# Attention with a soft mixture of experts: a new order table for all five instruction streams

## The chip, the cores and the metric

The kernel runs on one core of a Trainium2 chip. The metric is the device time of one execution in microseconds (us), smaller is better. The median of three runs of the kernel before is 386.3 us.

## The reference

```python
scores = scale * np.matmul(q, k.transpose(0, 1, 3, 2))      # 8 batches, 8 heads, 576 x 64
mask = block_i >= block_j                                   # blocks of 64 rows
scores = np.where(mask, scores, -1000000000.0)
attn = np.exp(scores - np.max(scores, axis=-1, keepdims=True))
attn = attn / (np.sum(attn, axis=-1, keepdims=True) + 1e-09)
x = np.matmul(attn, v)                                      # heads side by side: 4608 x 512
...
logits = x @ phi                                            # 4608 x 32
d = softmax of logits over the 4608 rows; c = softmax over the 32 slots
slot_input = d.T @ x                                        # 8 experts, 4 slots each
slot_out[e] = np.maximum(slot_input[e] @ w1[e], 0.0) @ w2[e]
out = c @ slot_out
```

All values are float32. The two `softmax` lines stand for the four written-out lines of each.

## The kernel before

The 8 batches have 8 heads each; two heads make a *pair*, so there are 32 pairs, numbered m = 0 to 31, four to a batch. The 576 rows of a head are nine blocks of 64, and because of the mask a block row needs only the columns up to its own block. The kernel calls the rows by their last block: tile 7 (blocks 6 and 7, 512 columns), tile 5 (blocks 4 and 5, 384 columns), and the *small blocks* 8, 3, 2, 1 and 0, which share banks.

What is done for pair m, with the engine, the function and the name that the order table uses:

- SP loads q, k and v (`lq`, `lk`, `lv`); POOL scales k (`ks`, L276).
- PE makes the scores: `UA` tile 7 (L312, 512 columns, into the banks sc0 and sc1), `UB` the small blocks (L333, into sc8, sc0 and sc1), `UC` tile 5 (L312, 384 columns, into sc8).
- DVE takes the row maxima out of these banks (`rm..`, L347), ACT exponentiates them into SBUF and adds up the rows (`ex..`, L357), DVE inverts the sums (`z0` to `z2`, L363 and L364), POOL multiplies (`nm..`, L369).
- PE transposes the probabilities into two banks, pt_e and pt_o (L386): `g7` (16 transposes), `gc` (block 8, 10), `gd` (blocks 3 to 0, 12), `g5` (12). Each of the four groups overwrites these two banks, so each waits until the group before has been copied out: by `eg7`, `og7`, `egc`, `ogc` and so on, e for pt_e and o for pt_o (L242 on ACT, L244 on DVE).
- PE multiplies by the values: `pa` for block 8 (L434, 64 columns; it needs `egc` and `ogc` alone), `pv0` and `pv1` for the rest (L424; they need all eight copies). Both go into bank x0, and are copied into xT by `xa` (64 columns) and `xb` (512 columns).

The work is software-pipelined. In one turn of the steady state PE runs UA of pair m, `g7` of pair m-1, `pv` of pair m-2, UB of pair m, then `gc`, `gd`, `g5` and `pa` of pair m-1 around UC of pair m. The destination of the copies out of pt_e and pt_o is not doubled, so `eg7` and `og7` wait until the `pv` of the pair before has ended.

Once per batch there is work of the expert part, spread over the four turns: logits `prt0` to `prt4` (L453, L463) and their copy `elg`, running maxima `stats` and exponentials `stats2`, two turned copies `nlt` and `ndt` (L497, L498) with their copies `enl` and `disp`, x turned back `xq0`, `xq1`, `xn4` (L553) with the copies `en0a` to `en4b`, and the sums `sl` (L571, 512 columns) and `sl4` (L580) with the updates `sacc` and `sacc4`. These go through the banks x0 and x1. Where they stand between `gc` and `gd` or after `g5` or `pa`, this text calls them fillers.

All instructions are written in an order that the table `TM` sets: each step of pair m has the time m x T + TM[name], each step of batch b the time 4 x b x T + TM[name], and the steps are recorded sorted by that time. The times set the order only; on the chip every engine runs its stream in that order, and waits on semaphores. Names with `w` belong to pair 30, with `y` to pair 31, with `z` to the last batch. The table `EN` says for each copy whether ACT ("a") or DVE ("v") makes it, and with an `X` name which of the banks x0 and x1 a step uses. `FILL` puts three dummy matmuls behind `pv1` of the last pair and behind the last `sl`.

After the pairs follow the merge into siT (L694 to L696), the expert matmuls (L792, L819), and the output (L770, ten DMAs). The weights come in 32 pieces of 1 MB: 15 while the pairs run, 17 after the last load of v, into memory that the pairs have given back.

Of the kernel before, what the change touches and what calls it, by code (L numbers as in the profile page):

```python
# [45 lines left out]
for name, n in (  # L46
# [12 lines left out]
W0 = NLATE * PIECE  # L59
STEPS = (2, 2, 3, 3, 3, 3, 0)  # L60
TM = {
# [8 lines left out]
    56.559, "prt4": 57.002, "elg": 57.036, "stats": 61.554, "stats2": 62.94, "nlt": 60.569, "enl": 64.437,  # L70
# [7 lines left out]
    177.171, "slz": 214.293, "sacc4z": 228.677, "saccz": 280.777, "enlz": 179.062, "disp2z": 157.986,  # L78
    "mg6z": 241.542, "comb0z": 79.04, "comb1z": 92.334, "lqw": -27.673, "lqy": -20.712, "lkw": -27.957,
    "lky": -32.568, "lvw": -2.375, "lvy": 21.104, "ksw": -25.397, "ksy": -27.683, "UAw": -19.276, "UAy":  # L80
    -18.528, "UBw": -14.362, "UBy": -14.986, "UCw": -8.47, "UCy": -3.006, "rm70w": -18.712, "rm70y":
# [11 lines left out]
    "eg5y": 42.092, "og5w": 10.671, "og5y": 42.312, "egcw": -0.404, "egcy": 24.728, "ogcw": -0.303, "ogcy":  # L93
    14.062, "egdw": 4.267, "egdy": 31.651, "ogdw": 5.622, "ogdy": 32.008, "paw": 7.714, "pay": 27.683,
    "xbw": 13.5, "xby": 52.045, "xaw": 10.034, "xay": 34.863, "pv0": 10.742, "pv1": 10.723, "pv0w": 12.719,
    "pv1w": 12.814, "pv0y": 43.045, "pv1y": 49.055,
}
EN = {
    "xa": "v", "xb": "v", "lg": "v", "n0a": "v", "n0b": "a", "n1a": "v", "n1b": "a", "n4a": "v", "n4b": "a",
    "nl": "v", "dn": "a", "eg7": "a", "og7": "a", "eg5": "a", "og5": "a", "egc": "a", "ogc": "v", "egd":  # L100
    "a", "ogd": "v", "Xpa": 0, "Xlg": 1, "Xnl": 1, "Xnd": 0, "Xn4": 1, "Xsi": 1, "Xsi4": 0, "Xpb": 0,
    "Xlgz": 1, "Xnlz": 1, "Xndz": 0, "Xsiz": 0, "lgz": "a", "nlz": "v", "dnz": "v", "n0az": "v", "n0bz":
    "a", "n1az": "v", "n1bz": "a", "n4az": "a", "n4bz": "a", "xay": "a", "xby": "a", "eg7y": "v", "og7y":
    "a", "eg5y": "a", "og5y": "v", "egcy": "a", "ogcy": "v", "egdy": "a", "ogdy": "v", "Xpay": 0,
}
FILL = {"pv1": 3, "slz": 3}
NB = B
# [810 lines left out]
```

## Time and profile before

| what | value |
|---|---|
| runs | 386.2, 386.3, 387.93 us; median 386.3 |
| profiled execution | 387.56 us, of which the span from the first to the last instruction is 385.8 |
| busy PE, DVE, ACT, POOL | 365.4, 286.7, 278.1, 182.0 us |
| PE busy from 60 to 290 us | 226.79 of 230 us |
| scores of the small blocks (UB) of pair 2, of pair 30 | start at about 27.9 and at about 294.5 us |
| siT begins, last output is issued | 326.97 and 380.59 us |
| granted TensorE clock, mean | 0.978 |

In a timeline each row has the start, the length (from the first start to the last end of a group), engine, line, operation, what is written and read, the shape and the count; in brackets the idle time before it and what ended it. A matmul of float32 stands as two records. Ends of matmuls are modelled, so the time that PE gives to a step is read here from its start to the start of the next step. On DVE and ACT an instruction may start before the one ahead of it has ended.

### The profile page before, as it was taken

The numbers are of one execution on the slowest core, as the hardware profiler recorded it, in microseconds if no ns is written. First come the engines' busy times: TensorE is split into PE (matmuls) and PEld (weight loads), VectorE is DVE, ScalarE is ACT, GpSimd is POOL, SyncE is SP. The second block draws the span as 40 slices with busy tenths as digits, with TensorE's granted clock in tenths as the row PEclk, the third lists the DMA queues.
The fourth block names the chain that finished last, engine by engine and source line by source line (L and its number), as shares of the span: only waits on it lengthen the run. The fifth ranks groups of instructions, "written<-read, shape, count | busy, mean of one in ns | idle before, by whom it ended". The sixth has DMA issues, their size and how long they took to land.

```text
span 385.8 us, 14041 instructions
## 1 busy us (share of the span) xinstructions
PE 365.4 (95%) x5487; PEld 241.8 (63%) x5487; DVE 286.7 (74%) x851; ACT 278.1 (72%) x883; POOL 182.0 (47%) x349
## 2 busy tenths in 40 slices
PE   7799999999999999999999999999999989999974
PEld 2466677667767776777667766766776655344542
DVE  3577779887988898889888988898889866041552
ACT  2687888988898889788888888888888854211441
POOL 5465665555555555555555555555555442010000
PEclk9699999999999999999999999999999999999995
DMA  5326366353564563535636635453332289799797
GB/s 158 93 63 209 108 216 197 101 203 98 199 206 105 201 197 98 211 92 197 216 92 211 198 102 194 119 187 97 93 95 65 88 305 358 297 426 406 290 373 329
DMA packets 28786, 72.27 MB, mean 187 GB/s; under 512 B 6832, under 2 KB 15152, under 8 KB 23600
## 3 DMA queue, kind: packets, MB, share of 16 engines
q1 hardware_dynamic: 28720, 71.38, 53.7%
q8 instruction: 43, 0.70, 0.7%
q14 instruction: 23, 0.19, 0.1%
HBM read 61.93 MB, written 9.44 MB: 185 GB/s over the span
## 4 chain that ended last, share of the span: by engine, by line
PE 89%; ACT 4%; DVE 3%; issue 2%; POOL 0%; ACTq 0%; POOLq 0%; DVEq 0%
PE x L424 19%; PE sc L312 16%; PE pt_e L386 11%; PE sc L333 11%; PE x L434 6%; PE pt_o L386 5%; PE so L819 4%; PE hp L792 4%; PE o L770 3%; PE x L553 3%; PE x L453 2%; PE x L571 2%; ACT arena L242 1%; PE x L283 1%; ACT arena L357 1%
## 5 line engine op out<-in xcount | busy, mean ns | idle before, releaser
L369 POOL TENSOR_SCALAR arena<-arena,stat 128x512 f32<-128x512 f32 (+6 forms) x288 | 152.6, 548 | 135.3 <-DVE stat L364 129.8
L357 ACT ACTIVATE arena<-sc,stat 128x512 f32<-128x512 f32 (+6 forms) x288 | 154.6, 550 | 20.9 <-DVE stat L347 18.5
L347 DVE TENSOR_REDUCE stat<-sc 128x1 f32<-128x512 f32 (+6 forms) x256 | 131.6, 541 | 4.3 <-PE sc L333 1.9
L386 PEld LDWEIGHTS pt_e<-ident,arena 64*128 64x128 f32 x800 | 63.7, 139 | 47.5 <-issue 30.9
L242 ACT COPY arena<-pt_e 128x384 f32<-128x384 f32 (+2 forms) x127 | 63.4, 500 | 24.2 <-PE pt_o L386 23.0
L386 PE MATMUL pt_e<-ident,arena 64*128 64x64 f32 x800 | 74.8, 228 | 5.0 <-ACT arena L242 3.5
L424 PE MATMUL x<-arena 128*64 128x256 f32 (+2 forms) x640 | 76.1, 384 | 0.4 <-DVE arena L244 0.4
L386 PE MATMUL pt_o<-ident,arena 64*128 64x64 f32 x800 | 74.7, 228 | 0.0
L312 PE MATMUL sc<-arena 64*128 64x512 f32 (+1 forms) x256 | 67.1, 598 | 0.8 <-ACT arena L357 0.7
L386 PEld LDWEIGHTS pt_o<-ident,arena 64*128 64x128 f32 x800 | 62.7, 139 | 0.2
L357 ACT ACTIVATION_READ_ACCUMULATOR arena<-sc,stat 128x1 f32 x288 | 61.2, 212 | 0.0
L424 PEld LDWEIGHTS x<-arena 128*64 128x64 f32 x640 | 41.0, 137 | 30.6 <-issue 18.2
L333 PE MATMUL sc<-arena 64*64 64x288 f32 (+4 forms) x768 | 45.7, 344 | 2.9 <-ACT arena L357 2.9
L333 PEld LDWEIGHTS sc<-arena 64*64 64x64 f32 x768 | 38.4, 134 | 12.1 <-issue 6.3
L242 ACT COPY arena<-pt_o 128x512 f32<-128x512 f32 (+1 forms) x63 | 33.8, 537 | 10.0 <-PE x L424 9.4
L244 DVE COPY arena<-pt_o 128x320 f32<-128x320 f32 (+1 forms) x65 | 33.9, 521 | 4.9 <-PE pt_o L386 3.0
L244 DVE COPY xT<-x 128x64 f32<-128x64 f32 (+1 forms) x42 | 19.0, 453 | 12.2 <-PE x L424 11.9
L363 DVE TENSOR_SCALAR stat<-stat 128x2 f32<-128x2 f32 (+1 forms) x96 | 26.4, 275 | 2.1 <-ACT arena L357 2.1
L434 PE MATMUL x<-arena 128*64 128x64 f32 x640 | 25.7, 227 | 0.0
L312 PEld LDWEIGHTS sc<-arena 64*128 64x128 f32 x256 | 20.6, 192 | 6.3 <-issue 2.4
L276 POOL TENSOR_SCALAR arena<-arena 128x576 f32<-128x576 f32 x32 | 21.6, 674 | 3.0 <-DMA arena<-in_k 3.0
L434 PEld LDWEIGHTS x<-arena 128*64 128x64 f32 x640 | 21.2, 137 | 2.2
(142 smaller groups left out, 343.8 us busy)
## 6 DMA issues: line engine op xcount, KB each, us to landing
arena<-in_w SPq DMA_DIRECT2D x32, 1024.0 KB, 6.7
arena<-in_k SPq DMA_DIRECT2D x32, 288.0 KB, 3.7
arena<-in_q SPq DMA_DIRECT2D x32, 288.0 KB, 3.0
arena<-in_v SPq DMA_DIRECT2D x32, 256.0 KB, 3.1
out<-arena SPq DMA_DIRECT2D x8, 1024.0 KB, 4.7
arena<-in_v SPq DMA_DIRECT2D x32, 32.0 KB, 2.7
out<-arena SPq DMA_DIRECT2D x2, 512.0 KB, 4.6
arena<-in_phi SPq DMA_DIRECT2D x1, 64.0 KB, 3.1
```

The source lines that it names most:

```text
L242: nc.scalar.copy(out=out, in_=in_)
L244: nc.vector.tensor_copy(out=out, in_=in_)
L276: nc.gpsimd.tensor_scalar(out=area(f"ks{m % NQB}"), in0=area("kr"), scalar1=SCALE, scalar2=0.0, op0=ALU.mult, op1=ALU.add)
L312: nc.tensor.matmul(scores(t + str(j)), lhsT=q[r, lo:lo + 128], rhs=k[r, 0:NC[t]], start=True, stop=True)
L333: nc.tensor.matmul(o, lhsT=a, rhs=b, start=True, stop=True)
L347: nc.vector.tensor_reduce(out=st[:, 0, u:u + n], in_=sc, axis=AX.XY if x == "8" else AX.X, op=ALU.max, negate=True)
L357: nc.scalar.activation(out=pr, in_=sc, func=AF.Exp, bias=st[:, 0, u:u + 1], accum_out=st[:, 1, u:u + 1],)
L363: nc.vector.tensor_scalar(out=st[:, 2, c], in0=st[:, 1, c], scalar1=EPS, scalar2=None, op0=ALU.add)
L369: nc.gpsimd.tensor_scalar(out=pr, in0=pr, scalar1=st[:, 2, u:u + 1], scalar2=0.0, op0=ALU.mult, op1=ALU.add)
L386: nc.tensor.transpose(out=ptb[i][:, 64 * n:64 * n + 64], in_=prob(m, x)[r, 128 * c:128 * c + 128], identity=ident[r, r],)
L424: nc.tensor.matmul(xps[m, 0][64 * j:64 * j + 64, lo:hi], lhsT=vs(m)[:, j, c, :], rhs=rhs, start=a, stop=z, skip_group_check=True,)
L434: nc.tensor.matmul(xps[m, 1][64 * j:64 * j + 64, 0:64], lhsT=vs(m)[:, j, c, :], rhs=arena[:, lo:lo + 64], start=(c == 0), stop=(c == NQ - 1),)
```

## The change

`TM` and `EN` get new numbers, and T goes from 13.5 to 9.2; nothing else is changed. The lines of the changed kernel are one lower than before (L385 is L386). No function, tile or buffer is added or removed, and every instruction of the one is in the other, but for the engine of some copies. A piece of the two tables:

```diff
-    "egc": 0.999, "ogc": -0.07, "gd": 3.63, "egd": 4.561, "ogd": 4.524, "g5": 5.41, "eg5": 8.642, "og5":
-    8.288, "pa": 6.153, "xb": 11.788, "xa": 7.179, "prt0": 41.378, "prt1": 41.386, "prt2": 43.082, "prt3":
+    "T": 9.2, "lq": 8.391, "lk": 5.062, "lv": 19.959, "ks": 6.651, "UA": 10.483, "UB": 13.066, "UC": 18.108,
+    "pa": 27.331, "xb": 31.614, "xa": 27.947, "prt0": 53.039, "prt1": 53.06, "prt2": 54.239, "prt3": 59.773,
...
-    "xa": "v", "xb": "v", "lg": "v", "n0a": "v", "n0b": "a", "n1a": "v", "n1b": "a", "n4a": "v", "n4b": "a",
-    "nl": "v", "dn": "a", "eg7": "a", "og7": "a", "eg5": "a", "og5": "a", "egc": "a", "ogc": "v", "egd":
-    "a", "ogd": "v", "Xpa": 0, "Xlg": 1, "Xnl": 1, "Xnd": 0, "Xn4": 1, "Xsi": 1, "Xsi4": 0, "Xpb": 0,
+    "xa": "a", "xb": "a", "lg": "a", "n0a": "a", "n0b": "a", "n1a": "a", "n1b": "v", "n4a": "a", "n4b": "a",
+    "nl": "a", "dn": "a", "eg7": "a", "og7": "v", "eg5": "v", "og5": "a", "egc": "a", "ogc": "v", "egd":
+    "v", "ogd": "v", "Xpa": 0, "Xlg": 1, "Xpb": 0, "Xnl": 0, "Xnd": 0, "Xsi": 1, "Xsi4": 0, "Xlgz": 1,
```

What moves to another engine in a turn: `og7`, `eg5` and `egd` from ACT to DVE, `xa` and `xb` from DVE to ACT; once per batch `elg`, `en0a`, `en1a`, `en4a` and `enl` go from DVE to ACT, and `en1b` from ACT to DVE. So tile 7 and tile 5 are copied out by one engine each for pt_e and pt_o, and both halves of `gd` by DVE.

PE in one turn of the steady state, before: the last transpose of `gd`, then UC into bank sc8, `g5`, `pa` into x0, and UA of the next pair.

```order
L386 MATMUL pt_o<-ident,arena 128x64
L312 MATMUL sc_104<-arena 128x384 x2
L386 MATMUL pt_e<-ident,arena 128x64
...
L386 MATMUL pt_o<-ident,arena 128x64
L434 MATMUL x_100<-arena 64x64 x10
L312 MATMUL sc_102<-arena 128x512
```

The same place of the changed kernel, in a turn in which `xq0` stands as a filler behind `g5`:

```order
L385 MATMUL pt_o<-ident,arena 128x64
L311 MATMUL sc_104<-arena 128x384 x2
L433 MATMUL x_100<-arena 64x64 x10
L385 MATMUL pt_e<-ident,arena 128x64
...
L385 MATMUL pt_o<-ident,arena 128x64
L552 MATMUL x_100<-ident,xT_109 128x64
...
L311 MATMUL sc_102<-arena 128x512
```

The ten matmuls of `pa` have moved from behind the transposes of `g5` to ahead of them.

DVE in one turn, before (in a turn with the updates `sacc4` and `disp2`): from `xb` (the copy of x_100 into xT) over `z0`, the maximum of block 8 out of sc_104, `ogc`, the maxima of blocks 0, 1 and 2, `ogd`, to the maximum of block 3.

```order
L244 COPY xT_112<-x_100 128x512
L363 TENSOR_SCALAR stat_107<-stat_107 128x2
L364 RECIPROCAL stat_107<-stat_107 128x2
L347 TENSOR_REDUCE stat_107<-sc_104 128x1
L244 COPY arena<-pt_o 128x320
L347 TENSOR_REDUCE stat_107<-sc_102 128x1
L592 SCALAR_TENSOR_TENSOR acc_76<-acc_76,bm_1572,x_100 128x128
L512 TENSOR_TENSOR zrun<-zrun,bm_1572 128x2
L513 TENSOR_TENSOR zrun<-zrun,bm_1572 128x2
L347 TENSOR_REDUCE stat_107<-sc_103 128x1 x2
L244 COPY arena<-pt_o 128x384
L347 TENSOR_REDUCE stat_107<-sc_102 128x1
```

DVE in one turn of the changed kernel, one without updates, from `z0` to `eg5`:

```order
L362 TENSOR_SCALAR stat_107<-stat_107 128x2
L363 RECIPROCAL stat_107<-stat_107 128x2
L243 COPY arena<-pt_o 128x2x4x64
L346 TENSOR_REDUCE stat_107<-sc_104 128x1
L243 COPY arena<-pt_o 128x320
L346 TENSOR_REDUCE stat_107<-sc_102 128x1 x2
L346 TENSOR_REDUCE stat_107<-sc_103 128x1 x2
L243 COPY arena<-pt_o 128x384
L243 COPY arena<-pt_e 128x384
L342 MEMSET sc_104 64x2x64
L346 TENSOR_REDUCE stat_107<-sc_104 128x2
L243 COPY arena<-pt_e 128x2x3x64
```

`og7` has taken the place of `xb`, all four small maxima stand ahead of `ogd`, `egd` follows it, and `eg5` follows the maximum of tile 5. On ACT the turn was `og7`, `eg7`, `egc`, `ex8` and is `eg7`, `xb`, `egc`, `ex8`.

The fillers by turn, counted from the turn that begins with the logits `prt0`: between `gc` and `gd` stood `sl4` with `prt0` to `prt2`; `prt3`, `prt4` (and `xq0` behind `gd`, `nlt` behind `pa`); `ndt` (and `xq1` behind `gd`); `xn4` ahead of `gc` with `sl` behind it. Now stand there `ndt` with `prt0` to `prt2`; `prt3`, `prt4`, `sl4` (and `xn4` behind `g5`); `nlt`, `sl` (and `xq0` behind `g5`); `xq1`.

PE at the end of the pairs, before: `pv1` of the last pair, the dummies, `prt3`, `prt4`, `xq0`, `nlt` of the last batch.

```order
L424 MATMUL x_100<-arena 64x128 x2
L290 MATMUL sc_102<-idle 128x512
...
L453 MATMUL x_101<-xT_110,arena 32x128 x4
L463 MATMUL x_101<-xT_111,arena 32x64 x4
...
L553 MATMUL sc_102<-ident,xT_111 128x64
...
L497 MATMUL x_101<-ident,lt_5331 128x128
```

The same place of the changed kernel:

```order
L423 MATMUL x_100<-arena 64x128 x2
L289 MATMUL sc_102<-idle 128x512
...
L452 MATMUL x_101<-xT_110,arena 32x128 x4
L579 MATMUL x_100<-xn,dn 32x128 x4
L462 MATMUL x_101<-xT_111,arena 32x64 x4
...
L552 MATMUL sc_102<-ident,xT_111 128x64
...
L570 MATMUL x_101<-xn,dn 32x512 x4
L496 MATMUL x_100<-ident,lt_5310 128x128
```

`sl4` (L579) and `sl` (L570) of the batch before the last now stand inside the last chain of steps. Because the expert part trails further behind, the turn of pair 30 also holds `sl` of the batch before that one and `nlt` and `xq0` of batch 6, and no longer `ndt`; `xn4` of batch 6 now stands ahead of it. The load of phi is now the first DMA of SP's queue, and the first weight piece stands behind the second load of q, ahead of the first load of v.

More of the change, by code (lines that the diff above doesn't have):

```diff
@@ L61 @@
 TM = {
[8 rows of a table removed]
-    56.559, "prt4": 57.002, "elg": 57.036, "stats": 61.554, "stats2": 62.94, "nlt": 60.569, "enl": 64.437,
[7 rows of a table removed]
[L78 to L81, printed above, removed]
[11 rows of a table removed]
@@ L93 @@
[L93 to L96, printed above, removed]
[10 rows of a table added]
+    "enl": 71.336, "stats2": 73.971, "ndt": 88.52, "disp": 90.039, "sl": 106.532, "sacc": 109.619, "sl4":
[6 rows of a table added]
+    55.302, "comb1z": 59.886, "lqw": 6.269, "lqy": 10.133, "lkw": 0.332, "lky": -0.691, "lvw": 24.288,
@@ L97 @@
+    "lvy": 21.795, "ksw": 4.334, "ksy": 5.55, "UAw": 10.635, "UAy": 10.72, "UBw": 12.532, "UBy": 12.589,
[12 rows of a table added]
+    27.69, "ogcw": 23.896, "ogcy": 24.626, "egdw": 25.932, "egdy": 28.643, "ogdw": 26.551, "ogdy": 29.889,
+    "paw": 26.386, "pay": 28.961, "xbw": 33.288, "xby": 32.843, "xaw": 27.216, "xay": 29.983, "pv0": 30.892,
+    "pv1": 30.898, "pv0w": 29.715, "pv1w": 29.523, "pv0y": 32.401, "pv1y": 32.627,
 }
 EN = {
-    "xa": "v", "xb": "v", "lg": "v", "n0a": "v", "n0b": "a", "n1a": "v", "n1b": "a", "n4a": "v", "n4b": "a",
@@ L100 @@
-    "nl": "v", "dn": "a", "eg7": "a", "og7": "a", "eg5": "a", "og5": "a", "egc": "a", "ogc": "v", "egd":
-    "a", "ogd": "v", "Xpa": 0, "Xlg": 1, "Xnl": 1, "Xnd": 0, "Xn4": 1, "Xsi": 1, "Xsi4": 0, "Xpb": 0,
-    "Xlgz": 1, "Xnlz": 1, "Xndz": 0, "Xsiz": 0, "lgz": "a", "nlz": "v", "dnz": "v", "n0az": "v", "n0bz":
-    "a", "n1az": "v", "n1bz": "a", "n4az": "a", "n4bz": "a", "xay": "a", "xby": "a", "eg7y": "v", "og7y":
-    "a", "eg5y": "a", "og5y": "v", "egcy": "a", "ogcy": "v", "egdy": "a", "ogdy": "v", "Xpay": 0,
+    "xa": "a", "xb": "a", "lg": "a", "n0a": "a", "n0b": "a", "n1a": "a", "n1b": "v", "n4a": "a", "n4b": "a",
```

53 rows, old and new, of tables (EN, TM) are left out of this document.

## The prediction

> **What bounds the kernel now.** I read the busy times of the steady stretch first, then the chain that ended last, then PE's timeline, then those of DVE and ACT.
>
> ```profile
> 60.00:290.00 230.00, 226.79 (x3692) 159.11 (x3692) 198.03 (x590) 195.10 (x639) 129.64 (x240) 1.00 0.48 154
> ```
>
> The columns are PE, PEld, DVE, ACT and POOL. PE is busy for 226.79 of 230 us at full clock: PE sets the pace, and an order can gain only what PE loses between its steps. DVE (198.03, 86%) and ACT (195.10, 85%) are near enough to be late.
>
> ```profile
> 27.89 1.25 PE sc L333 x15
> ...
> 47.85 0.79 PE x L453 x24
> ...
> 217.95 1.45 PE sc L333 x16
> ...
> 256.19 1.45 PE sc L333 x17
> ...
> 294.45 1.37 PE sc L333 x14
> ```
>
> These rows of the chain mark UB of pairs 2, 22, 26 and 30. Four turns took 256.19 - 217.95 = 38.24 us, the 28 turns from pair 2 to pair 30 266.56. One turn without fillers, on PE:
>
> ```profile
> 36.88 1.32 PE L333 MATMUL sc<-arena 64*64 64x288 f32 x24
> 38.27 0.24 PE L386 MATMUL pt_e<-ident,arena 64*128 64x64 f32 x1
> ...
> 39.34 0.27 PE L386 MATMUL pt_e<-ident,arena 64*128 64x64 f32 x1 [0.54 <-ACT arena L242]
> ...
> 40.07 0.92 PE L312 MATMUL sc<-arena 64*128 64x384 f32 x4
> 40.83 0.24 PE L386 MATMUL pt_e<-ident,arena 64*128 64x64 f32 x1
> ...
> 41.34 0.80 PE L434 MATMUL x<-arena 128*64 128x64 f32 x20
> 42.07 1.13 PE L312 MATMUL sc<-arena 64*128 64x512 f32 x4
> ...
> 45.93 0.70 PE L333 MATMUL sc<-arena 64*64 64x288 f32 x8
> ```
>
> Start to start, UB takes 1.39, UC 0.76, `g5` 0.51, `pa` 0.73, and UA, `g7` and `pv` together 3.86. Between `gc` (38.27) and `gd` (39.34) PE waits for the copies of `gc`. The other two engines beside that:
>
> ```profile
> 38.12 0.76 DVE L347 TENSOR_REDUCE stat<-sc 128x1 f32<-128x576 f32 x1
> 38.90 0.49 DVE L244 COPY arena<-pt_o 128x320 f32<-128x320 f32 x1
> 39.31 0.68 DVE L347 TENSOR_REDUCE stat<-sc 128x1 f32<-128x64 f32 x3
> 40.07 0.56 DVE L244 COPY arena<-pt_o 128x384 f32<-128x384 f32 x1
> 40.54 0.41 DVE L347 TENSOR_REDUCE stat<-sc 128x1 f32<-128x256 f32 x1
> ```
>
> ```profile
> 38.85 0.43 ACT L242 COPY arena<-pt_e 128x320 f32<-128x320 f32 x1 [0.73 <-PE pt_o L386]
> 39.18 0.75 ACT L357 ACTIVATE arena<-sc,stat 128x576 f32<-128x576 f32 x1
> 39.81 0.20 ACT L357 ACTIVATION_READ_ACCUMULATOR arena<-sc,stat 128x1 f32 x1
> ...
> 46.59 0.59 ACT L242 COPY arena<-pt_e 128x512 f32<-128x512 f32 x1
> ```
>
> UC (40.07) starts 0.06 after `ex8` has read its sum (39.81 + 0.20): both use bank sc8. And `gc` waits for `eg7`: by the second pair's rows `eg7` ends at 46.59 + 0.59 = 47.18, 1.25 after its UB. Follow-on instructions start about 0.08 us ahead of the end of the one before (39.31 is 0.08 before 38.90 + 0.49).
>
> **The change part by part.** The prices of the fillers, and UB where nothing holds up what follows it:
>
> ```profile
> 265.50 1.32 PE L333 MATMUL sc<-arena 64*64 64x288 f32 x24
> 266.75 0.34 PE L553 MATMUL x<-ident,arena 64*128 64x64 f32 x4
> ...
> 267.05 0.22 PE L386 MATMUL pt_e<-ident,arena 64*128 64x64 f32 x1
> ...
> 267.70 1.07 PE L571 MATMUL x<-xn,dn 128*32 128x512 f32 x8 [0.18 <-ACT xn L242]
> 268.70 0.27 PE L386 MATMUL pt_e<-ident,arena 64*128 64x64 f32 x1
> ...
> 269.12 0.87 PE L312 MATMUL sc<-arena 64*128 64x384 f32 x4
> ```
>
> ```profile
> 259.14 0.35 PE L553 MATMUL x<-ident,arena 64*128 64x64 f32 x4
> ...
> 259.64 0.92 PE L312 MATMUL sc<-arena 64*128 64x384 f32 x4
> ...
> 308.92 0.92 PE L312 MATMUL sc<-arena 64*128 64x384 f32 x4
> 309.76 2.38 PE L424 MATMUL x<-arena 128*64 128x256 f32 x20
> ...
> 320.50 0.42 PE L453 MATMUL x<-xT,arena 128*32 128x128 f32 x8
> 320.75 0.63 PE L463 MATMUL x<-xT,arena 128*32 128x64 f32 x32
> 321.31 0.72 PE L553 MATMUL sc<-ident,xT 64*128 64x64 f32 x16
> 321.95 0.33 PE L497 MATMUL x<-ident,lt 128*128 128x128 f32 x1
> ...
> 322.32 0.71 PE L553 MATMUL sc<-ident,xT 64*128 64x64 f32 x16
> ```
>
> UB 1.25; `xn4` 0.30; `gc` 0.47 (267.05 to 267.70 less the wait of 0.18); `sl` 1.00; `gd`, and `g5` where transposes follow, 0.42; `xq0` or `xq1` 0.50; UC followed by values instead of transposes 0.84; `prt3` 0.25, `prt4` 0.56, `nlt` or `ndt` 0.37; `prt0` to `prt2` 0.79 (from the chain). For `sl4` I take the 0.25 of `prt3`, which has as many matmuls of the same width.
>
> *UB to `gc`.* `eg7` now runs on ACT beside `og7` on DVE, so both end about 0.8 us after UB's start instead of 1.25, and `gc` starts at 1.25 rather than 1.39. `xb` on ACT fits behind `eg7` (to 1.3), ahead of `egc` (1.83).
>
> *`gc` to UC.* DVE (times from UB's start): maximum of block 8 at 1.24, `ogc` 1.92 to 2.41, four small maxima to 3.26 (0.60 for three, 0.33 for one, less the overlaps). ACT: `egc` 1.83, `ex8` 2.16 to 2.99. So `gd` can't start before 2.41, nor UC before 3.05. PE reaches UC at 1.25 + 0.47 + fillers + 0.42, which is 3.30, 3.20, 3.51 and 2.64 in the four kinds of turn (fillers 1.16, 1.06, 1.37, 0.50); the last waits until 3.05.
>
> *`pa` ahead of `g5`.* `pa` needs only `egc` and `ogc`, long done. It puts 0.84 + 0.73 = 1.57 instead of 0.76 between the start of UC and `g5`, as cover for the copies of `gd`; UC itself costs 0.08 more. The price is that both copies are on DVE: `ogd` 0.47, `egd` 0.55, from 3.26 or from `gd`'s end. Without updates they end by 4.5, `g5` comes at 4.6 to 4.9: covered. In the second kind `sacc4` and `disp2` stand ahead of them (0.66 from 277.67 to 278.33):
>
> ```profile
> 277.67 0.34 DVE L592 SCALAR_TENSOR_TENSOR acc<-acc,bm,x 128x128 f32<-128x128 f32 x1
> ...
> 278.33 0.55 DVE L347 TENSOR_REDUCE stat<-sc 128x1 f32<-128x128 f32 x2
> ```
>
> `egd` then ends at 3.26 + 0.66 + 0.47 + 0.55 = 4.94, and `g5` waits 0.17. In the third kind `sacc` does about the same, but PE is at `g5` at 5.08 only: 0.14 to spare. If the overlap of 0.08 on DVE were gone, this cover would be too.
>
> *POOL and UA.* POOL is busy for 129.64 of 230 us, 0.54 an instruction (129.64 / 240). From `z2` on, about 0.4 ahead of UB, it now has `nm50`, `ks`, `nm0`, `nm2`, then `nm70` and `nm71` of the next pair, then `nm51`: seven, done about 3.5 after UB. `gd` needs the fourth (1.8, comes at 2.4 at the earliest), `g5` the last (comes at 4.6): covered, but `nm51` now stands behind a wait for `z0` of the next pair, and a `z0` over 1 us late would hold `g5`. UA overwrites sc0 and sc1, so it waits for the exponentials of the small blocks; in the turn with `xq1`, ACT has `en1a` ahead of them, and they end at about the time PE comes to UA (estimate 5.0). At the turn with `stats`, DVE reaches `og7` about 0.5 after UB, ends it at about 1.2, and `gc` is just not held.
>
> *The turns.* Each is UC's start + 1.57 + 0.42 + filler behind `g5` + 3.86: 3.30 gives 9.15; 3.20, the wait and `xn4` 9.52; 3.51 and `xq0` 9.86; 3.05 8.90. Sum 37.43 against 38.24. The first six turns, with few fillers, are 4 x 8.90 + 9.20 + 9.40 = 54.20. Then follow 6, 6, 5 and 5 turns of the kinds, 205.82 together. Total 260.0 against 266.6: -6.5 us.
>
> *The end.* The expert part trails, so after pair 30's UB there is more work: `nlt` 0.37 + `sl` 1.00 + `xq0` 0.50 - `xn4` 0.30 = +1.6. Part of it falls into waits that PE has there anyway; in the last chain `sl4` puts `prt4` back by 0.25, and `sl` keeps PE from `ndt` for about 0.6. I take +0.9, between 0 and +2.
>
> *The start* I cost at nothing: phi ahead of k delays the loads by one issue of about half a microsecond (estimate), under PE's warm-up; at most +0.6. The weight piece ahead of v has 13 us until `pa` needs v. `lq` and `lk` wait for the same releases a turn ahead.
>
> *What the sum leaves out.* Three places a batch have 0.14 us or less to spare: `g5` behind `sacc`, UA behind `en1a`, `gc` behind `stats`. The trace before has no such place to price them by; the nearest row is the 0.18 that `sl` waits for ACT. I charge it once a batch, 0.2 in 7 batches: +1.4; the bounds are 0 and three times that, +4.
>
> Sum: -6.5 + 0.9 + 1.4 = -4.2 us, 383.4 for the profiled execution of 387.56. That one lies 1.3 above the median of the runs (386.3), so 382.1 is the forecast.
>
> **The rivals.** *VectorE falls behind (slower).* DVE gains two 384-column copies of 0.56 a turn, against `xa` and the batch's copies that leave: about 0.4 more (estimate), from 8.2 of 9.5 us to 8.6 of 9.3. All of its work from `og7` to `egd` is one chain ahead of `g5`. If that chain comes 0.6 later than I walk it, `g5` waits 0.25, 0.6, 0.46 and 0.26 more in the four kinds, 1.57 a batch or 11 us: 393. From 0.43 on the kernel is slower by over 0.5%. Against it speaks that DVE starts the chain with UB, whatever came before, and that the rows show the overlap between copies and maxima; for it, nine instructions at 0.08 of lost overlap would make 0.7.
>
> The Trainium skill's page "TensorEngine Tiling (Array Packing)", Performance Considerations, says of exactly this to "Use both ScalarE and VectorE for PSUM evacuation". By it `gd`'s copies in series would cost PE one copy, 0.47, in each of some 30 turns: 14 us, 396. No run here has shown the two in series yet.
>
> *The gain is eaten (no change).* The same chain 0.35 late costs 4 us and leaves 386. The waits then move from `gc` and `gd` to `g5`.
>
> *All waits go.* Without the charge, the end's extra work and the wait at `g5` (0.17 x 6), it is 386.3 - 6.5 - 1 = 378.8.
>
> *The order is not what runs.* The streams show the moves in every turn, so I give this no chance.
>
> **How the numbers follow.** A measurement of this kernel can tell about 0.5% (1.9 us) from no change. The forecast, 379.5 to 384.4, has 0.57; all waits gone 0.12; eaten 0.18; VectorE late 0.13. Faster 0.69, same 0.18, slower 0.13. The range from 378.5 to 388 leaves out the slower case and the far end of the fast one.
>
> **What would show it.** Right: four turns near 37.6 us; `gc` 1.25 after UB; UC of the turn with `xq1` at `ex8`'s end; `g5` waits for DVE's L243 in one turn of four at most. Wrong: `g5` or `g7` waits for DVE in most turns, DVE busy over 93%; or the time from pair 30's UB to siT (294.4 to 327 before) grows by more than 2 us.

## The result and the profile after

| | before | after |
|---|---|---|
| median of the runs (four of each) | 386.5 us | 380.5 us |
| profiled execution, its span | 387.56, 385.8 us | 380.48, 378.7 us |
| UB of pair 2 starts | 27.89 | 26.53 |
| UB of pair 2 to UB of pair 30 | 266.56 | 259.15 |
| UB of pair 30 to siT | 32.52 | 34.17 |

The ratio of the runs is 0.984, with a 95% interval of 0.982 to 0.987: 6 us less. Measured again later (experiment 10) it was 382.0 against 386.7 us, 0.987, or 4.7 us less. Where a run had an execution in the slower state of the chip (571.2 us in experiment 1, 398.5 us in experiment 3), its median leaves that out. The last three rows are starts in the chain of waits and, for siT, in PE's timeline; they add up to the difference of the spans: -1.36, -7.41 and +1.65 make -7.1.

The steady stretch of the changed kernel (columns PE, PEld, DVE, ACT, POOL, clock, DMA):

```profile
60.00:290.00 230.00, 228.00 (x3748) 153.69 (x3744) 201.90 (x600) 192.13 (x661) 133.38 (x249) 1.00 0.46 147
```

PE is at 228.00 where it was at 226.79, but in a stretch that now holds more of the work; DVE went from 198.03 to 201.90, 88%. The chain shows the turns better:

```profile
26.53 1.14 PE sc L332 x11
...
183.61 1.25 PE sc L332 x15
192.53 1.25 PE sc L332 x15
201.71 1.14 PE sc L332 x11
211.13 1.25 PE sc L332 x16
220.89 1.14 PE sc L332 x11
...
285.68 1.25 PE sc L332 x16
```

From 183.61 on these are UB of pairs 19 to 23: turns of 8.92 (with `xq1`), 9.18 (`prt0`), 9.42 (`sl4`) and 9.76 (`sl`), 37.28 together against 38.24. The turn with `xq1` on PE:

```profile
183.54 1.32 PE L332 MATMUL sc<-arena 64*64 64x288 f32 x24
184.79 0.27 PE L385 MATMUL pt_e<-ident,arena 64*128 64x64 f32 x1
...
186.62 0.92 PE L311 MATMUL sc<-arena 64*128 64x384 f32 x4
187.46 0.80 PE L433 MATMUL x<-arena 128*64 128x64 f32 x20
188.20 0.27 PE L385 MATMUL pt_e<-ident,arena 64*128 64x64 f32 x1
...
188.62 1.10 PE L311 MATMUL sc<-arena 64*128 64x512 f32 x4
```

`gc` starts 1.25 after UB, UC (186.62) 3.08 after it, `pa` 0.84 later, `g5` (188.20) without a wait. ACT says what UC waited for, the end of `ex8` at 186.36 + 0.20:

```profile
185.73 0.75 ACT L356 ACTIVATE arena<-sc,stat 128x576 f32<-128x576 f32 x1
186.36 0.20 ACT L356 ACTIVATION_READ_ACCUMULATOR arena<-sc,stat 128x1 f32 x1
```

and DVE why `g5` needn't wait: `ogd` and `egd`, one behind the other, end at 187.78.

```profile
186.77 0.54 DVE L243 COPY arena<-pt_o 128x384 f32<-128x384 f32 x1
187.24 0.54 DVE L243 COPY arena<-pt_e 128x384 f32<-128x384 f32 x1
```

Two turns later, in the one with `sl4`, `egd` ends at 206.40, and `g5` starts at 206.46, 0.14 after `pa` would have let it:

```profile
205.85 0.55 DVE L243 COPY arena<-pt_e 128x384 f32<-128x384 f32 x1
```

```profile
205.58 0.80 PE L433 MATMUL x<-arena 128*64 128x64 f32 x20
206.46 0.27 PE L385 MATMUL pt_e<-ident,arena 64*128 64x64 f32 x1
```

That is the only place where `g5` waits. The four kinds of turn, in us from the start of UB, means of six turns each out of PE's timeline (the first of kind 2 after has no `sl` yet; the five with `sl` have 3.49, 5.95 and 9.76 after):

| kind, by what stands ahead of UC (before; after) | UC before | UC after | next UA before | after | next UB before | after |
|---|---|---|---|---|---|---|
| 0: `sl4`, `prt0`-`prt2`; `ndt`, `prt0`-`prt2` | 3.28 | 3.30 | 5.53 | 5.25 | 9.39 | 9.18 |
| 1: `prt3`, `prt4`, `xq0`; `prt3`, `prt4`, `sl4` | 3.69 | 3.15 | 6.01 | 5.49 | 9.87 | 9.42 |
| 2: `ndt`, `xq1`; `nlt`, `sl` | 3.52 | 3.42 | 5.51 | 5.89 | 9.38 | 9.70 |
| 3: `xn4`, `sl`; `xq1` | 3.63 | 3.08 | 5.75 | 5.08 | 9.61 | 8.92 |

With the prediction's prices (UB 1.25, `gc` 0.47, `gd` 0.42 and the fillers) PE's own work from UB to UC was 3.18, 3.45, 3.01, 3.44 before, so that it waited 1.04 us in four turns; now it is 3.30, 3.20, 3.51, 2.64, and 0.44 is waited in kind 3, nothing elsewhere. From UC to UA (2.00 without a wait and a filler) PE waited 0.25 before in kind 0 and 0.13 in kind 3, for the copies of `gd`; now only the 0.14 of kind 1 is there. Together that is 0.84 of the 0.97 us that four turns with `sl` have won; the rest lies in small differences of the prices.

The end, from `prt3` of the last batch on:

```profile
311.90 0.42 PE L452 MATMUL x<-xT,arena 128*32 128x128 f32 x8
312.14 0.40 PE L579 MATMUL x<-xn,dn 128*32 128x128 f32 x8
312.36 0.63 PE L462 MATMUL x<-xT,arena 128*32 128x64 f32 x32
312.92 0.72 PE L552 MATMUL sc<-ident,xT 64*128 64x64 f32 x16
313.57 1.07 PE L570 MATMUL x<-xn,dn 128*32 128x512 f32 x8
314.56 0.33 PE L496 MATMUL x<-ident,lt 128*128 128x128 f32 x1
...
319.85 0.46 PE L693 MATMUL siT_ps<-fident,acc 128*128 128x128 f32 x2 [0.20 <-DVE acc L586]
```

`prt3` to `nlt` (L496) was 1.45 (320.50 to 321.95), and is 2.66, with `sl4` (L579) and `sl` (L570) between; `prt3` to siT was 6.47 and is 7.95.

### The profile page after: what moved, and what is told of

Its sections match the earlier page's. It is cut to its first block, busy times and chain, and to the rows that moved or that the text cites. A ratio compares the mean times of both kernels' runs of the same rounds, so it can differ in the third digit from the quotient of the medians.

```text
span 378.7 us, 14017 instructions
## 1 busy us (share of the span) xinstructions
PE 359.7 (95%) x5487; PEld 232.2 (61%) x5487; DVE 287.6 (76%) x845; ACT 268.0 (71%) x889; POOL 180.5 (48%) x349
## 4 chain that ended last, share of the span: by engine, by line
PE 84%; DVE 9%; ACT 4%; issue 2%; POOL 0%; ACTq 0%; POOLq 0%; DVEq 0%
PE x L423 20%; PE sc L311 14%; PE pt_e L385 12%; PE sc L332 10%; PE x L433 5%; DVE stat L346 4%; PE so L818 4%; PE o L769 4%; PE hp L791 4%; ACT arena L356 3%; DVE arena L243 2%; PE pt_o L385 2%; PE x L570 2%; PE x L452 2%; PE x L552 1%
## 5 line engine op out<-in xcount | busy, mean ns | idle before, releaser
L356 ACT ACTIVATE arena<-sc,stat 128x512 f32<-128x512 f32 (+6 forms) x288 | 152.9, 545 | 15.5 <-DVE stat L346 13.5
L346 DVE TENSOR_REDUCE stat<-sc 128x1 f32<-128x512 f32 (+6 forms) x256 | 128.3, 542 | 17.6 <-PE sc L332 15.5
L385 PEld LDWEIGHTS pt_e<-ident,arena 64*128 64x128 f32 x800 | 60.3, 139 | 38.6 <-DVE arena L243 18.6
L385 PE MATMUL pt_e<-ident,arena 64*128 64x64 f32 x800 | 75.9, 229 | 4.4 <-ACT arena L241 3.6
L423 PE MATMUL x<-arena 128*64 128x128 f32 (+2 forms) x640 | 76.1, 384 | 0.4 <-DVE arena L243 0.4
L385 PE MATMUL pt_o<-ident,arena 64*128 64x64 f32 x800 | 75.9, 230 | 0.1
L311 PE MATMUL sc<-arena 64*128 64x512 f32 (+1 forms) x256 | 64.8, 583 | 1.7 <-ACT arena L356 1.2
L385 PEld LDWEIGHTS pt_o<-ident,arena 64*128 64x128 f32 x800 | 60.2, 139 | 0.4 <-DVE arena L243 0.3
L243 DVE COPY arena<-pt_o 128x384 f32<-128x384 f32 (+2 forms) x96 | 54.5, 568 | 3.0 <-PE pt_o L385 2.0
L241 ACT COPY arena<-pt_e 128x512 f32<-128x512 f32 (+1 forms) x65 | 33.0, 508 | 30.5 <-PE pt_o L385 24.4
L243 DVE COPY arena<-pt_e 128x384 f32<-128x384 f32 (+1 forms) x63 | 34.3, 545 | 0.4 <-PE pt_o L385 0.3
L362 DVE TENSOR_SCALAR stat<-stat 128x2 f32<-128x2 f32 (+1 forms) x96 | 18.5, 193 | 11.3 <-ACT arena L356 11.0
L778 DVE COPY arena<-o 128x512 f32<-128x512 f32 (+1 forms) x20 | 12.1, 634 | 13.6 <-PE o L769 13.4
```

What stands on the lines that cost most here:

```text
L241: nc.scalar.copy(out=out, in_=in_)
L243: nc.vector.tensor_copy(out=out, in_=in_)
L311: nc.tensor.matmul(scores(t + str(j)), lhsT=q[r, lo:lo + 128], rhs=k[r, 0:NC[t]], start=True, stop=True)
L346: nc.vector.tensor_reduce(out=st[:, 0, u:u + n], in_=sc, axis=AX.XY if x == "8" else AX.X, op=ALU.max, negate=True)
L356: nc.scalar.activation(out=pr, in_=sc, func=AF.Exp, bias=st[:, 0, u:u + 1], accum_out=st[:, 1, u:u + 1],)
L362: nc.vector.tensor_scalar(out=st[:, 2, c], in0=st[:, 1, c], scalar1=EPS, scalar2=None, op0=ALU.add)
```

## The experiments

My theory: a turn is PE's own chain, and the new order takes its waits out: `pa` covers the two copies of `gd` in series, the copies of tile 7 side by side let `gc` begin with the end of UB, and the fillers stand where no copy is missing. Each run undoes one of these, or does one alone in the kernel before. Times are medians; ratios are to the kernel before on the same chip, with 95% intervals. "28 turns" is UB of pair 2 to UB of pair 30 (266.56 before, 259.15 after), "four turns" the sum of the means of the four kinds (38.25 and 37.22).

**1. `pa` back behind `g5`, in the changed kernel.**

```diff
-    "pa": 27.331, "xa": 27.947, "og5": 28.482
+    "pa": 27.94, "xa": 27.96, "og5": 27.95
```

> The changed kernel (380.5 us) with pa put back behind g5 in the steady turns (xa moves behind og5); the copies of gd stay on DVE. My theory, that pa is the cover which lets ogd and egd run in series on DVE: g5 then comes 0.76 after the start of UC and waits for egd in every turn. By the trace of the changed kernel egd ends 4.52, 4.76, 4.83 and 4.24 after UB in the four kinds of turn, and g5 would be there at 4.06, 3.91, 4.18 and 3.84: waits of 0.46, 0.85, 0.65 and 0.40, less 4 x 0.08 for UC and the 0.14 that is waited there now, +1.9 us in four turns, 39.1 instead of 37.2, about +13 us: 393 to 394. The rival, that the place of pa is indifferent and the gain comes from the division of the copies alone: 380.5, no wait at g5 that is longer than now.

Measured: 405.5 us, ratio 1.049 (1.045 to 1.052); 28 turns 281.5, four turns 40.54. In a turn of kind 0 UC starts at 210.36, and `g5` waits for `egd`:

```profile
210.36 0.87 PE L311 MATMUL sc<-arena 64*128 64x384 f32 x4
...
211.64 0.27 PE L385 MATMUL pt_e<-ident,arena 64*128 64x64 f32 x1 [0.41 <-DVE arena L243]
```

Kinds 0 and 3 grew by 0.51 and 0.49, near the 0.38 and 0.32 expected; kinds 1 and 2 by 1.14 and 1.19. There a second wait stands that I had overlooked: `xn4` and `xq0` write bank x0 behind `g5`, and wait until `pa`'s result has been copied out by `xa`, which in my edit stood behind `og5` on top. So `pa` ahead of `g5` covers `xa` too, and the rival is out; how much of that second wait comes of the place of `xa` alone is left open.

**2. `pa` ahead of `g5`, alone, in the kernel before.**

```diff
-    "g5": 5.41, "pa": 6.153
+    "g5": 5.9, "pa": 5.85
```

> The kernel before (386.5 us) with pa ahead of g5 in the steady turns, and nothing else. My theory: where one copy of gd is on ACT and one on DVE there is little for pa to cover. It removes g5's wait of about 0.12 in two kinds of turn, and puts in a wait of pa for the copies of xq0 and xq1 out of bank x0 of about 0.17 in the two others: four turns 38.3 as before, 386.5 to 387.3. The rival, that pa ahead of g5 is a gain by itself: at least the 0.23 in four turns that g5 waits now, and up to 1 us in four turns if that was where the change won, 380 to 385.

Measured: 395.4 us, ratio 1.024 (1.020 to 1.027); four turns 39.28. Worse than either expectation. The waits of `pa` in kinds 1 and 2 are there as expected, but so is one that I had not thought of. ACT copies `og5` and `eg5` one after the other, and ends at 209.10:

```profile
208.24 0.48 ACT L242 COPY arena<-pt_o 128x384 f32<-128x384 f32 x1 [0.27 <-PE pt_o L386]
208.62 0.48 ACT L242 COPY arena<-pt_e 128x384 f32<-128x384 f32 x1
```

```profile
208.07 1.13 PE L312 MATMUL sc<-arena 64*128 64x512 f32 x4
209.25 0.24 PE L386 MATMUL pt_e<-ident,arena 64*128 64x64 f32 x1
```

UA (208.07) to `g7` (209.25) is 1.18 instead of 0.96. Behind `g5`, `pa` was the cover for *these* copies. Moved ahead, it covers those of `gd`.

**3. The same with the copies of `g5` side by side.** If that reading is right, `eg5` on DVE takes the wait at `g7` away.

```diff
-    "g5": 5.41, "pa": 6.153, "eg5": 8.642      "eg5": "a"
+    "g5": 5.9, "pa": 5.85, "eg5": 7.15         "eg5": "v"
```

> The kernel before (386.5 us) with pa ahead of g5, as in the run that came to 395.4 us, and besides with eg5 on DVE behind the maximum of tile 5, so that the two copies of g5 are made side by side as in the changed kernel. My theory: pa behind g5 was the cover for eg5 and og5 in series on ACT; with pa ahead of g5 there is UA alone, 0.96, and g7 waited 0.2 to 0.3 in three kinds of turn. Side by side they need no cover: that wait goes, the wait of pa for the copies of xq0 and xq1 stays. Four turns 38.55 (39.28 in that run, 38.25 in the kernel before), about 388.5. The rival, that pa ahead of g5 costs this by its waits for bank x0 alone: 39.3 in four turns, 395.

Measured: 392.9 us, ratio 1.014 (1.012 to 1.017); four turns 38.82, between the two expectations and nearer to mine; 28 turns 270.6, which is +4.1, and another 1.4 us arise between UB of pair 30 and siT (34.40 instead of 32.98 in the chain), where the last pairs have an order of their own.

```profile
206.58 1.13 PE L312 MATMUL sc<-arena 64*128 64x512 f32 x4
207.57 0.25 PE L386 MATMUL pt_e<-ident,arena 64*128 64x64 f32 x1
```

UA to `g7` is 0.94 to 0.99 in all kinds of turn. What stays is the wait of `pa` for the copies of `xq0` and `xq1` out of x0, and a late `gc` (1.64) in kind 2.

**4. The copies of tile 7 on one engine again, in the changed kernel.**

```diff
-    "eg7": "a", "og7": "v", "xb": "a"
+    "eg7": "a", "og7": "a", "xb": "v"
```

> The changed kernel (380.5 us) with the copies of tile 7 both on ACT again, as before the change: eg7, og7, and xb on DVE. My theory: og7 ends at about 1.25 instead of 0.7 after UB, gc starts at 1.39 instead of 1.25; in the turn with xq1 UC is bound by ex8 and nothing is lost, in the turn with sl4 g5 waits for egd anyway and nothing is lost, in the other two 0.14 each: four turns 37.5 instead of 37.2, about +2 us, 382.5. Rival: no change, 380.5.

Measured: 382.7 us, ratio 0.990 (0.987 to 0.993); four turns 37.42, 28 turns 260.4, +1.3. The size is near, the reason is not: `gc` still starts 1.25 after UB.

```profile
201.67 0.58 ACT L241 COPY arena<-pt_e 128x512 f32<-128x512 f32 x1 [0.25 <-PE x L423]
202.15 0.59 ACT L241 COPY arena<-pt_o 128x512 f32<-128x512 f32 x1
```

```profile
201.72 1.32 PE L332 MATMUL sc<-arena 64*64 64x288 f32 x24
202.97 0.27 PE L385 MATMUL pt_e<-ident,arena 64*128 64x64 f32 x1
```

The second copy ends at 202.74, 1.02 after UB, ahead of `gc`. In the kernel before the first one began 0.17 after UB, here 0.05 ahead of it; the order of `pv0` and `pv1` differs too, and which of the two it is was not tried. What is lost in every batch is lost in kind 2, where the second copy ends at 1.30 and UC comes 0.11 later (3.60 instead of 3.49): about half of the 1.3. The other half are two single turns, one of kind 3 and one of kind 1, 0.24 and 0.37 longer than the others of their kinds. In the second of them `ogc` came late, after 0.28 on DVE in which the profile shows it waiting for nothing:

```profile
241.37 0.49 DVE L243 COPY arena<-pt_o 128x320 f32<-128x320 f32 x1 [0.28 <-issue]
```

Another 0.8 is lost between UB of pair 30 and siT (35.01 instead of 34.17 in the chain).

**5. The copies of tile 7 side by side, alone, in the kernel before**, twice. In the first run the time of `xb` in the table was left as it was, so that it stood ahead of `eg7` on ACT, other than the expectation says; the second has it behind.

```diff
-    "og7": "a", "xb": "v"
+    "og7": "v", "xb": "a"
-    "xb": 11.788
+    "xb": 12.3
```

> The kernel before (386.5 us) with the copies of tile 7 divided as in the changed kernel: og7 on DVE in the place of xb, xb on ACT behind eg7. My theory: gc starts 1.25 after UB instead of 1.39 to 1.45 in three kinds of turn; of that nothing is left in the turn with prt0 to prt2, where g5 then waits longer for ogd, and nothing is won in the turn where xn4 stands ahead of gc; the other two win 0.14 and 0.2. Four turns 37.9 instead of 38.25, about -2.4 us: 384. Rival: the copies of tile 7 are hidden, no change, 386.5.

> The kernel before (386.5 us) with og7 on DVE in the place of xb and xb on ACT, this time behind eg7 (in the run before this one xb stood ahead of eg7, which then ended 1.19 after UB instead of about 0.7). My theory, now that the changed kernel with both copies of tile 7 on ACT lost only 0.2 us in four turns: gc starts at 1.25 instead of 1.39 and 1.45 in three kinds of turn, and half of that is lost again to g5's wait for ogd: four turns 38.0 instead of 38.25, about -1.5 us, 385. The rival, that nothing comes of it: 386.4, as in the run with xb ahead of eg7 (38.15).

Measured: 386.4 us, ratio 0.999 (0.997 to 1.001), four turns 38.15; and 385.9 us, ratio 0.998 (0.996 to 1.000), four turns 38.22. In the second `gc` does start at 1.25 in kinds 0 and 1, and UC 0.14 earlier; in kind 0 `g5` waits for `ogd` all the same, and its turn is 9.40 as before. In kinds 2 and 3 nothing is won ahead of UC. 28 turns take 265.9 instead of 266.6, half of what I had. The rival is nearly right: in that order the copies of tile 7 are hidden.

**6. `xq1` behind `g5`, in the changed kernel.**

```diff
-    "xq1": 78.923, "en1a": 81.356
+    "xq1": 83.2, "en1a": 84.3
```

> The changed kernel (380.5 us) with xq1 (and its copy en1a) moved from between gc and gd to behind g5. My theory: in the turn with xq1 UC is bound by the end of ex8, 3.02 after UB, and not by PE, so PE waits there for as long as xq1 took, and xq1 costs its 0.50 behind g5 in full: that turn 9.4 instead of 8.92, four turns 37.7, about +3.5 us, 384. The rival, that a filler costs the same wherever it stands: 380.5.

Measured: 385.1 us, ratio 0.990 (0.987 to 0.994); the turn with `xq1` 9.40, the others as they were, four turns 37.70. As my theory had it: UC stays at 3.08, at the end of `ex8`, and PE waits there as long as `xq1` took.

**7. `egd` back on ACT, in the changed kernel.**

```diff
-    "egd": "v"
+    "egd": "a"
```

> The changed kernel (380.5 us) with egd on ACT again, so that the two halves of gd are copied out by DVE and ACT side by side. My theory: the copies in series are covered by pa, so only the wait of 0.14 at g5 in the turn with sl4 goes; the copy of 0.5 on ACT puts back the exponentials of the small blocks, and UA, which overwrites their banks, then waits about 0.4 in the turn with xq1: four turns 37.5, about +2 us, 382.5. The rival, by which a copy on its own engine is worth its time in each turn (0.47 x 28 turns): about 368. Halfway, if only the wait goes: 379.5.

Measured: 385.7 us, ratio 0.994 (0.991 to 0.997); four turns 37.64. Kind 3 lost 0.43, the others 0.06 or less either way. The size is the one expected, the place is not UA but `g5`: ACT has `en1a` ahead of the exponentials in this turn, and comes to `egd` only behind three of them. The wait of 0.14 in kind 1, which was to go, stays: in the turn of pair 21 `egd` on ACT ends at 209.34 + 0.51 = 209.85, and `g5` starts at 209.90. Another 1.0 is lost between UB of pair 30 and siT (35.15 instead of 34.17 in the chain). `egd` keeps its time in the table here; an earlier place on ACT was not tried.

```profile
191.18 0.51 ACT L241 COPY arena<-pt_e 128x384 f32<-128x384 f32 x1
```

```profile
190.58 0.80 PE L433 MATMUL x<-arena 128*64 128x64 f32 x20
191.75 0.27 PE L385 MATMUL pt_e<-ident,arena 64*128 64x64 f32 x1 [0.36 <-ACT arena L241]
```

**8. One copy more on DVE, in the changed kernel.** `ogd` is made twice.

```diff
             copy("eo"[i] + g, dst, src, late(m))
+            if g == "gd" and i and not late(m):
+                copy("eo"[i] + g, dst, src)
```

> The changed kernel (380.5 us) with ogd made twice in the steady turns, which puts one more copy of 0.48 on DVE ahead of egd and changes nothing else. My theory, in which the margin between DVE's chain and g5 is 0.3, 0, 0.13 and 0.4 in the four kinds of turn: g5 waits 0.17, 0.43, 0.36 and 0.08 more, 1.04 in four turns, about +7 us, 388: one copy more on DVE gives the whole gain back. The rival, that DVE, busy for 88%, has room for it: 380.5.

Measured: 399.0 us, ratio 1.027 (1.024 to 1.031); four turns 39.48, 28 turns 274.9: +15.7, twice what I had reckoned.

```profile
208.15 1.15 DVE L243 COPY arena<-pt_o 128x384 f32<-128x384 f32 x2 [0.18 <-PE pt_o L385]
209.22 0.55 DVE L243 COPY arena<-pt_e 128x384 f32<-128x384 f32 x1
```

```profile
209.82 0.27 PE L385 MATMUL pt_e<-ident,arena 64*128 64x64 f32 x1 [0.28 <-DVE arena L243]
```

The second copy costs 0.59, not 0.48. `g5` starts 0.33, 0.59, 0.52 and 0.23 later in the four kinds, 1.67, and the four turns grow by 2.26. The rest is a second wait, of 0.25 and 0.31, at `g7` in kinds 0 and 3, from UA 1.23 instead of 0.98 and 0.91: `eg5` stands behind the maximum of tile 5 on DVE, and that behind `egd`.

**9. The end without the sums of the batch before the last, in the changed kernel.**

```diff
             for key, (fn, *args) in misc.items():
+                if b == NB - 2 and key in ("sl", "sacc", "sl4", "sacc4"):
+                    continue
```

> The changed kernel (380.5 us) without sl, sl4, sacc and sacc4 of the batch before the last, so that this batch is missing in the sums of the experts' inputs. My theory of the end: sl4 stands ahead of prt4 and sl ahead of nlt in the last chain, and stats2 overwrites what nlt reads, so both cost their whole time, 0.25 and 0.92: from the start of UB of pair 30 to siT 33.0 us instead of 34.2, the span 1.2 shorter. The rival, by which most of it falls into waits that PE has there anyway (the prediction had 0.6 for the two in the chain): 0.3 to 0.6 shorter.

Measured, one execution: 381.05 us, span 379.3. UB of pair 30 starts at 287.08 and siT at 319.98:

```profile
287.08 1.25 PE sc L332 x15
```

```profile
319.98 0.38 PE L695 MATMUL siT_ps<-fident,acc 128*128 128x128 f32 x2 [0.42 <-DVE acc L586]
```

32.90, 1.27 less than 34.17: both cost their whole time, as my theory had it, but not by way of `stats2`. In the profile of the changed kernel ACT and DVE stand still until `sl` (L570) is through. On ACT it is a copy of `xq0` into xn, which has one buffer and which `sl` still reads; on DVE it is `sacc`, and the other copy of `xq0` stands behind it.

```profile
314.67 0.59 ACT L241 COPY xn<-sc 128x512 f32<-128x512 f32 x1 [1.29 <-PE x L570]
```

```profile
314.73 0.75 DVE L586 SCALAR_TENSOR_TENSOR acc<-acc,bm,x 128x512 f32<-128x512 f32 x1 [0.52 <-PE x L570]
```

`stats2` follows on ACT at 315.15, behind that copy and without a wait. (The 1.49 in the next expectation was read to the end of the last `sacc` instead of the start of siT.) The span alone doesn't show the 1.27, because this execution's start was 1.4 longer (below) and its part behind siT 0.4.

**10. A better end and a freer kind 1, and the changed kernel again beside it.**

```diff
-    "disp2": 100.936
+    "disp2": 102.31, "sl4u": 96.65, "sacc4u": 96.7, "slu": 97.04, "saccu": 97.2
-FILL = {"pv1": 3, "slz": 3}
+FILL = {"slz": 3}
-            p0 = xbank("si", endz(b))
+            p0 = xbank("si", endz(b)) if b != NB - 2 else scn[:, 512:1024]
-            p0 = xbank("si4") if b < NB - 1 else scn[:, 0:512]
+            p0 = xbank("si4") if b < NB - 2 else scn[:, 0:512]
-                at(t0 + TM[key + "z" if b == NB - 1 else key], fn, b, *args)
+                at(t0 + (TM[key + "z"] if b == NB - 1 else TM.get(key + "u" * (b == NB - 2), TM[key])), fn, b, *args)
```

> The changed kernel (380.5 us) with two moves. sl4 and sl of the batch before the last leave the last chain: sl4 stands behind prt2 of the last batch, sl behind the last pv1 in place of the three dummy matmuls, both into the free bank pair sc8. And disp2 stands behind eg5, instead of ahead of ogd and egd. My theory: without these sums the time from UB of pair 30 to siT was 1.49 shorter; sl behind pv1 puts prt3 back by about 0.35, so 1.1 is left; and g5's wait of 0.14 in the turn with sl4 goes, 0.9 us in all: 378.5. The rival, that the chip has nothing left there (a sum moved is a sum paid elsewhere): 380.5.

> The changed kernel again, on the same chip as the three above, to stand beside them: 0.984 of the kernel before, four turns 37.2. Its start tells on the granted clock: by my theory UB of pair 2 starts at about 25.6 us if the clock isn't lowered between 10 and 20 us, and at about 27.5 if it is at half for 5 us; by the rival, that the new order shortened the start, at 26.5 in any case.

Measured: 379.3 us, ratio 0.979 (0.977 to 0.982), against 382.0 us, 0.987 (0.985 to 0.989), for the changed kernel on the same chip: 2.7 us less, with intervals that don't touch. `sl` (L570) now stands at 311.41 in the place of the dummies, and from UB of pair 30 (285.94) to siT it is 32.89, as if these sums cost nothing:

```profile
311.41 1.06 PE L570 MATMUL sc<-xn,dn 128*32 128x512 f32 x8
...
318.83 0.46 PE L693 MATMUL siT_ps<-fident,acc 128*128 128x128 f32 x2 [0.18 <-DVE acc L586]
```

With `disp2` behind `eg5` kind 1 falls from 9.42 to 9.17, by the wait of 0.14 at `g5` and by another 0.11 behind UA. The other kinds are as they were, but for a single turn of kind 2 that took 10.13 instead of 9.77; 28 turns 258.1.

**The start.** The profiled execution of the changed kernel reached UB of pair 2 at 26.53 instead of 27.89. The second profile of the same kernel shows 27.93, and this row for its first turns (the last columns are clock, DMA share and GB/s):

```profile
10.00:20.00 10.00, 8.26 (x65) 6.20 (x67) 6.21 (x21) 5.60 (x19) 4.38 (x8) 0.66 0.43 142
```

The first profile of the changed kernel, then the kernel before:

```profile
10.00:20.00 10.00, 6.98 (x66) 4.78 (x63) 6.88 (x21) 6.07 (x21) 5.38 (x11) 0.83 0.55 176
```

```profile
10.00:20.00 10.00, 8.24 (x67) 5.23 (x68) 6.04 (x20) 6.00 (x21) 5.07 (x10) 0.66 0.29 86
```

The run of experiment 4, with the start of the changed kernel, and the first of experiment 5, with that of the kernel before, had the full clock:

```profile
10.00:20.00 10.00, 6.92 (x86) 4.49 (x80) 7.15 (x22) 7.18 (x24) 6.25 (x12) 1.00 0.56 173
```

```profile
10.00:20.00 10.00, 6.34 (x85) 4.16 (x79) 7.97 (x23) 6.60 (x23) 6.62 (x12) 1.00 0.34 92
```

They reach UB of pair 2 at 25.95 in the chain and at 25.96 in PE's timeline (which has 25.88 for the first of the two):

```profile
25.95 1.25 PE sc L332 x16
```

```profile
25.96 1.21 PE L333 MATMUL sc<-arena 64*64 64x288 f32 x21
```

At a clock of 1.00, 0.83 and 0.66 it is about 25.95, 26.5 and 27.9 with either order (for 0.83 with the order of before: 26.59 in PE's timeline, second run of experiment 5): the 1.36 at the start is the clock's, 0.3 to 0.4 later than my figures for the ends, and the rival is out. The share of the clock is not all that sets this time: with other orders of the first turns it was 27.2 and 26.9 at 0.83 (experiments 1 and 2), and 27.8 and 28.9 at 0.54 (experiments 3 and 8). At an equal clock the spans are 385.8 and 380.3, a difference of 5.5.

## Why the prediction was right, and where it was not

It had 382.1 us, in a range from 378.5 to 388.0; it was 380.5, and 382.0 when measured again. Its sum for the profiled execution was -4.2; at equal clock it is -5.5. That the sum is so near is in part luck: the turns won 0.9 more than it had and a charge of 1.4 did not come, but the end cost 0.75 more.

- *The turns* held. It had 9.15, 9.52, 9.86 and 8.90, measured were 9.18, 9.42, 9.76 and 8.92; 54.20 for the first six, measured 54.17; 260.0 for 28 turns, measured 259.15. The 0.1 in kinds 1 and 2 is nearly all that differs.
- *`gc` to UC* held: UC of the turn with `xq1` is at the end of `ex8` (3.08, predicted 3.05), and experiment 6 shows that PE has nothing to do there.
- *`pa` ahead of `g5`* held, with its one wait (0.14, predicted 0.17). But the prediction did not say what `pa` had covered in its old place. Experiments 2 and 3 show it: the copies of `g5`. The change can afford this because `eg5` and `og5` run side by side now. The step gave the right number by luck, because UA happens to cover one copy.
- *UB to `gc`* gave the right start (1.25), but not for the reason that holds in the changed kernel. It put the 0.14 down to the two engines. In the kernel before they do bring `gc` to 1.25 in two kinds of turn (experiment 5), and 0.7 us of the 28 turns; but experiment 4 has one engine and the same start. In the changed kernel the division of tile 7's copies is worth 0.1 in every four turns, not 0.14 in every turn.
- *What the sum leaves out*: the +1.4 for the thin margins didn't come. Turns of a kind agree within 0.01 from batch to batch in the profiled execution, so a margin of 0.13 or 0.14 was enough there. It is not always: single turns of experiments 4 and 10 were 0.24 to 0.37 longer than the others of their kind. This is the largest of the mis-sized terms.
- *The end* was mis-sized: +0.9 taken, +1.65 measured, inside its bounds of 0 to +2. The step that failed is "sl keeps PE from ndt for about 0.6". The copies of `xq0` wait for the whole of `sl`, on ACT because it still reads xn and on DVE behind `sacc` (experiment 9); with `sl4` that is 1.27 where the prediction had 0.85. The other 0.38 is a turn of pair 30 that is 0.76 longer in the chain (295.74 - 285.68 = 10.06, before 303.75 - 294.45 = 9.30), a stretch from there to `prt3` that is 0.59 shorter, and 0.21 between `prt3` and siT; what makes these was not tested.
- *The start* at nothing was right, and the profile alone would have said otherwise.
- *VectorE falls behind* did not come, but its price was too low: for 0.6 late it had 11 us, and 0.59 cost 15.7 (experiment 8), since it counted the wait at `g5` and not that at `g7`. The kernel sits closer to that edge than I thought.
- The rule of the Trainium skill's page "TensorEngine Tiling (Array Packing)", Performance Considerations, to use both engines for evacuation, was the rival with 396. It did not hold for `gd`: both copies on DVE lose 0.14 in one turn of four, not 0.47 in each, and dividing them again, with `egd` at its place in the table, made the kernel 0.7% to 1% slower (0.994 against 0.984 and 0.987). For the copies of `g5`, which have no such cover, it does hold: experiments 2 and 3.

None of the parts tried makes the gain alone. In the 28 turns `pa` first alone costs 7.5 us, and the division of tile 7 alone brings 0.7; undone one at a time in the changed kernel, the parts cost 1.3 us (tile 7), 2.9 (`xq1`), 2.8 (`egd`) and 22 (`pa`) of the 28 turns. Of the fillers only `xq1` was moved back, and the division of tile 5's copies was not undone in the changed kernel; what these are worth there is open.

## What to carry to other kernels

A step that needs nothing is cover: before moving it, ask which copies it hides where it stands, and which it will hide, and let an engine's serial copies stand where the cover is longest. A wait that the profile shows at one place is worth only what the next wait behind it leaves; walk the chain to the end of the turn before pricing a removal. And compare starts at an equal granted clock before giving a difference to an edit.

## What the runs showed of the chip

The granted clock between 10 and 20 us was 1.00, 0.83 or 0.66 in executions of one and the same start. Taken as half speed for a part of these 10 us, that is 0, 3.4 and 6.8 us, and it moved the pairs by 0.6 and 1.95 us. The Trainium skill's page "TensorE: Matmul & The Clock Gate", section "What's actually happening", describes a free-running window of 3413 ns in which the array goes between half and full clock. The steps seen here are none, one and two of these windows, so the traces agree.

Two identical copies of 384 columns back to back on DVE, out of one bank and into the same place, took 1.15 us (experiment 8), where `ogd` and `egd`, out of two banks, took 187.78 - 186.77 = 1.01: the overlap of 0.08 that the prediction counted on was there between copies of different banks (0.07), and not between these two. Which of bank and place it hangs on was not tried.
